# Retention and a SwiGLU feed-forward on one core: where the block sums of the gate and value weights are made, where their rounding keeps its scratch, and which engine writes two diagonals

## The chip, the cores and the metric
The kernel runs on one core of a Trainium2 chip. A core has five engines with a queue of their own each: TensorE (PE, with the load of its weights shown apart as PEld), VectorE (DVE), ScalarE (ACT), GpSimd (POOL) and SyncE (SP), which here does nothing but issue transfers. Every engine works off its instructions in the order in which the program lists them, and waits for others by semaphores. The metric is the device time of one execution in microseconds; less is better.

## The reference
Eight batches of eight heads: a retention block (attention without softmax, with a decay for each head), whose result goes as 4608 rows of 512 into a feed-forward block.

```python
scores = scale * np.matmul(q, k.transpose(0, 1, 3, 2))          # q, k, v: (8, 8, 576, 64)
ret = scores * Dmat[None, :, :, :]                              # decay gamma**(i - j) below the diagonal
x = np.matmul(ret, v).astype(np.float32)                        # then (B*S, H*D) = (4608, 512)
rms = np.sqrt(np.mean(x * x, axis=-1, keepdims=True) + 1e-06)
xn = x / rms * rms_g
g = xn @ w_gate                                                 # (512, 1536)
val = xn @ w_val
return (g * (1.0 / (1.0 + np.exp(-g))) * val @ w_out).astype(np.float32)
```
Of the inputs, the three weight matrices arrive as 64-bit floating point numbers, that is, as two 32-bit words each.

## The kernel before
**Units.** The 4608 rows are nine units of 512. For each, attention makes x (four head pairs, one "job" each: `turn` or `prepare`, `scores`, `states`, `weigh`, `sums`, then `values` and `carried`), a norm follows, then the products with gate and value weights ("up") and those with the output weights (`across`). From the third unit on (`up`, L609), an up product of 2 x 2 blocks takes seven block products in place of eight, which needs four sums of the weight's blocks: S1 to S4, beside A11, A12, A22. Units 0 and 1 (`up_plain`, L668) use the four plain blocks A11, A12, A21, A22 and no sums; they run while the weights are still being prepared.

**Rounding.** [...] They come in 36 halves (L853): 24 of the gate and value weights (six sets of four blocks) and 12 of the output weights (three slices of four). `load_half` brings one half of 512 KB raw into one of `N_RAW` places (three in the ring, two in other buffers). Then, on DVE: `exponent` (L896, one operation), two ScalarE operations (L889), `mantissa` (L911, L915, L919) and `join` (L936), which writes the rounded block. `exponent` of the next half stands ahead of `mantissa` of this one. `weights(n)` lists the next n of these steps; three make a half. In the first seven steps the scratch lies in SBUF; then `in_psum` is set (L1098), and the exponent and the masked high word each take one of the eight PSUM banks. The banks go round in the order of their allocation: who takes one waits for the last user of that bank, eight allocations back. `up_plain` takes one bank for each of its steps (eight matmul instructions), and the evictions by DVE (L685) or ScalarE (L687) free it.

**Sums and stores.** When a set's fourth half is joined, `finish_set` (L949) has POOL make the four sums (`combine_blocks`, L947) in a place behind the sets, and lists the stores of seven blocks to `w_up_d` in DRAM, to be issued by SP a few halves later. `finish_slice` does two levels of the like for the output weights (eight POOL operations).

**The ring.** One buffer of 17408 words for each partition. In `start` it holds the second unit's hidden values, three sets, the sums and three raw places; later the weights of `across` and `up`, streamed from DRAM as "pieces". `refill` (L574) issues a piece on SP as soon as the pieces that it overlaps have been listed as used; the transfer itself waits until they have been read. SP also issues the q, k, v loads of the jobs (`fetch`) and the stores of the output (`store`), all in program order.

**The norm of units 0 and 1.** `norm_1` (L467): four small matmuls and POOL's power give 1/rms for each row; `diagonals` (L480) writes it onto four diagonals by DVE; `scale_x` (L537) spreads them by one matmul into a bank (`rb`) and scales x by four DVE operations. `scale_first` (L265) has POOL scale q and v of the first eight jobs.

The order around this in `start`: four slots of jobs 0 to 3 with a few rounding steps between, the norm of unit 0, the slot of job 4, then 48 steps of `up_plain` in the hand-written order of L1100, with jobs 5 to 7, the norm of unit 1 and three rounding steps at each step (`now` counts them), and `across(0)`, `across(1)`. Then the loop over units 2 to 8 (L1185).

Of the kernel before, what the change touches and what calls it, by code (L numbers as in the profile page):

```python
# [14 lines left out]
P = 128  # L15
# [30 lines left out]
def kernel(  # L46
# [87 lines left out]
    h_1 = ring[:, : NF * U].rearrange("p (f t) -> p f t", t=U)  # L134
    BLOCK = 2 * 2 * P
    AT_SETS, N_SETS = NF * U, 3
    AT_SUMS = AT_SETS + N_SETS * 4 * BLOCK
    AT_RAW = AT_SUMS + 4 * BLOCK
    WORDS = 2 * 4 * P
    assert AT_RAW + 3 * WORDS <= RING  # L140
# [12 lines left out]

# [326 lines left out]
    def diagonals(u):  # L480

        r = t_of[u]
        t_of[u] = row(f"diag_{u}")
        for s in range(NS):
            nc.vector.tensor_scalar(
                out=t_of[u][:, s * P : s * P + P], in0=ident, scalar1=r[:, s : s + 1],
                scalar2=None, op0=ALU.mult,
            )

    def root_1(u):  # L490
# [64 lines left out]


    UP, OUT = 7 * 2 * 2 * P, 7 * NK * P
    w_up_d = dram.tile([2 * NG, P, UP], F32, name="w_up_blocks")
    w_out_d = dram.tile([7, NK, P, 7 * P], F32, name="w_out_blocks")
    ORDER = (A11, S1, S3, S2, A12, S4, A22)  # L560
    pieces = [("out", u, n) for u in range(2) for n in range(7)]
    for u in range(2, NU):
        pieces += [("up", u, n) for n in range(2 * NG)] + [("out", u, n) for n in range(7)]
    places = []
    at = AT_SUMS
    for kind, u, n in pieces:
        size = UP if kind == "up" else OUT
        if at + size > RING:
            at = AT_SETS if kind == "out" and u < 2 else 0
        places.append((at, at + size))  # L570
        at += size
    n_sent = n_used = 0

    def refill(most=len(pieces)):  # L574

        nonlocal n_sent
        while n_sent < min(most, len(pieces)):
            a, z = places[n_sent]
# [9 lines left out]
            nc.sync.dma_start(out=o, in_=src)  # L588
            n_sent += 1

    def piece(kind, u, n):
        assert pieces[n_used] == (kind, u, n) and n_used < n_sent
        a, z = places[n_used]
        if kind == "up":
            return ring[:, a:z].rearrange("p (b c f) -> p b c f", b=7, c=2)
        return ring[:, a:z].rearrange("p (c n d) -> p n c d", n=7, c=NK)

    def used():
        nonlocal n_used
# [68 lines left out]
    def up_plain(u, k):  # L668


        m, f = k % 2, k // 2 * 2
        hh = h_1 if u else h
        w = set_of(k)
        for half in range(2):
            for i in range(2):
                ps = bank(f"up_{u}_{k}_{half}_{i}")
                for c in range(NHP):
                    blk = (A21, A22)[c // 2] if half else (A11, A12)[c // 2]
                    nc.tensor.matmul(  # L679
                        ps, lhsT=w[:, PLACE[blk], c % 2, i * P : i * P + P],  # L680
                        rhs=x_of[u][:, c], start=(c == 0), stop=(c == NHP - 1),
                    )
# [208 lines left out]

    def exponent(i):

        exps[i] = bank(f"exp_{i}") if in_psum else flat_t[i % 2][:, WORDS:]
        w, e = words_of(i), exp_of(i).bitcast(U32)
        nc.vector.tensor_scalar(  # L896
            out=e, in0=w[:, 1::2], scalar1=20, scalar2=0x7FF,
            op0=ALU.logical_shift_right, op1=ALU.bitwise_and,
        )
        f = exp_of(i)  # L900
        acts.extend((i, x) for x in (
            dict(out=f, in_=e, bias=most, scale=-1.0),
            dict(out=e, in_=f, bias=top, scale=-(2.0**23)),
        ))

    def mantissa(i):
# [8 lines left out]
        nc.vector.tensor_scalar(  # L915
            out=m, in0=hi, scalar1=0xFFFFF, scalar2=0x100000,
            op0=ALU.bitwise_and, op1=ALU.bitwise_or,
        )
        nc.vector.scalar_tensor_tensor(  # L919
            out=lo.bitcast(F32), in0=lo, scalar=2.0**-32, in1=m, op0=ALU.mult, op1=ALU.add  # L920
        )

    def join(i):
# [2 lines left out]
        x, e = words_of(i)[:, 0::2].bitcast(F32), exp_of(i)  # L926
        if kind == "up":
            blk = ((A11, A12), (A21, A22))[a][c]
            cuts = [(set_of(k)[:, PLACE[blk]].rearrange("p c f -> p (c f)"), x, e)]
# [18 lines left out]

    def finish_set(k):  # L949
        w = set_of(k)  # L950
        s = ring[:, AT_SUMS : AT_SUMS + 4 * BLOCK].rearrange("p (b c f) -> p b c f", b=4, c=2)
        combine_blocks(
            {i: (w[:, n] if i in (A11, A12, A22, A21) else s[:, n - 3]) for i, n in PLACE.items()},
            A21,
        )
        stores.append((n_joined + 3, [
            (o, t.rearrange("p b c f -> p (b c f)"))
            for o, t in ((w_up_d[k][:, : 3 * BLOCK], w[:, :3]), (w_up_d[k][:, 3 * BLOCK :], s))
        ]))

    def finish_slice(k):
# [10 lines left out]
                nc.sync.dma_start(out=o, in_=t)  # L972

    stores = []
    in_psum = False
    n_joined = 0
    due = False
    sets_used = [0] * 2 * NG
# [44 lines left out]


    def start():

        nonlocal in_psum
# [13 lines left out]
        for j in range(FIRST):  # L1041
# [22 lines left out]
        for j in range(NHP):  # L1064
# [105 lines left out]
        for i, _ in enumerate(across(1)):  # L1170
# [70 lines left out]
```

## Time and profile before
| | |
|---|---|
| runs (4) | median 1157.88 us, 1154.86 to 1160.65 |
| the profiled execution | 1157.71 us, of which the span is 1155.7 us |
| mean granted TensorE clock | 0.982 |
| PE busy | 1105.4 us, 96% |
| PEld busy | 917.8 us, 79% |
| DVE busy | 819.9 us, 71% |
| POOL busy | 426.2 us, 37% |
| ACT busy | 242.6 us, 21% |
| DMA | 249.23 MB, mean 216 GB/s |

The span runs from the first instruction to the last. Its stages: to 53.5 us the first loads, jobs 0 to 4 and the norm of unit 0; to 268 us the plain products of units 0 and 1 with the rounding (done on DVE at 214.5 us); to 344 us `across(0)` and `across(1)`; to about 427 us the up products of the third unit; then the remaining units, each alike. A page row of waits names the engine and line that waited, who released it, the total time, how often, and the longest. Durations of a group are minimum, median and maximum in nanoseconds. The chain that ended last holds only the end of the last unit's combining on DVE (1145 to 1153 us).

### The profile page before, as it was taken

Reading aid. Unit: us, or ns where it says so; the run is one execution under the profiler, and the core shown is the slowest. Engines: PE = TensorE matmul, PEld = TensorE weight load, DVE = VectorE, ACT = ScalarE, POOL = GpSimd, SP = SyncE. Lnnn points to the kernel's source line nnn. Section 1 sums busy time; section 2 is a strip of 40 time slices with the busy share of each in tenths; the row PEclk is TensorE's granted clock in tenths of the full one; section 3 lists DMA queues with packets and bytes.
Section 4 is the critical chain, followed back from the end, with each engine's and each line's share of the span. In section 5 each row is a group of like instructions: output and inputs, shape, how many; then the busy total and the mean of one; then the engine's idle time right before and its main releaser. Section 6 shows DMA issues by size and latency. Waiting matters only on the chain. (4 is left out here: it accounts for less than half of the span.)

```text
span 1155.7 us, 24188 instructions
## 1 busy us (share of the span) xinstructions
PE 1105.4 (96%) x10086; PEld 917.8 (79%) x10086; DVE 819.9 (71%) x1402; ACT 242.6 (21%) x497; POOL 426.2 (37%) x356
## 2 busy tenths in 40 slices
PE   7697999898999999999999999999999999999997
PEld 6453443457998889888988899889988998898897
DVE  3877999466796779577947795779576944593465
ACT  3252453111012130123012301221212111201110
POOL 4522654405652018301740164006500660174035
PEclk9799999898999999999999999999999999999999
DMA  8726889459897887587767974788576566475461
GB/s 194 193 55 179 297 306 285 123 161 297 282 345 239 237 236 259 161 212 209 265 214 212 240 269 183 184 221 303 203 179 223 192 223 216 145 276 174 160 237 39
DMA packets 255612, 249.23 MB, mean 216 GB/s; under 512 B 193296, under 2 KB 214032, under 8 KB 249360
## 3 DMA queue, kind: packets, MB, share of 16 engines
q1 hardware_dynamic: 253776, 247.11, 68.4%
q8 instruction: 79, 1.29, 0.5%
q10 hardware_dynamic: 1728, 0.58, 0.2%
q14 instruction: 29, 0.24, 0.1%
HBM read 217.58 MB, written 30.08 MB: 214 GB/s over the span
## 5 line engine op out<-in xcount | busy, mean ns | idle before, releaser
L730 POOL TENSOR_TENSOR vi<-h 128x384 f32<-128x384 f32 x64 | 79.5, 1259 | 515.1 <-DVE h L637 454.0
L679 PE MATMUL up<-x,ring 128*128 128x512 f32 x384 | 173.5, 608 | 10.4 <-DVE ring L936 9.0
L618 PE MATMUL x<-x,ring 128*128 128x256 f32 x672 | 161.5, 383 | 0.0
L618 PE MATMUL w<-sums,ring 128*128 128x256 f32 x672 | 159.3, 380 | 0.0
L618 PE MATMUL z<-x,ring 128*128 128x256 f32 x672 | 158.7, 379 | 0.0
L679 PEld LDWEIGHTS up<-x,ring 128*128 128x128 f32 x384 | 72.7, 193 | 103.6 <-issue 85.5
L618 PEld LDWEIGHTS z<-x,ring 128*128 128x128 f32 x672 | 127.7, 190 | 19.9 <-issue 2.9
L618 PEld LDWEIGHTS w<-sums,ring 128*128 128x128 f32 x672 | 127.3, 190 | 17.4
L618 PEld LDWEIGHTS x<-x,ring 128*128 128x128 f32 x672 | 125.1, 190 | 17.5
L618 PE MATMUL y<-sums,ring 128*128 128x256 f32 x336 | 79.4, 379 | 0.0
L625 DVE TENSOR_TENSOR h<-u,w 128x512 f32<-128x512 f32 x42 | 28.9, 687 | 66.0 <-PE w L618 62.9
L831 POOL TENSOR_TENSOR vi<-vi 128x512 f32<-128x512 f32 (+1 forms) x56 | 67.2, 1213 | 22.2 <-DVE vi L777 19.7
L618 PEld LDWEIGHTS y<-sums,ring 128*128 128x128 f32 x336 | 63.8, 190 | 8.7
L625 DVE TENSOR_TENSOR u<-m,y 128x512 f32<-128x512 f32 x42 | 28.8, 685 | 49.8 <-PE y L618 49.8
L644 ACT COPY m<-x 128x512 f32<-128x512 f32 x42 | 24.6, 586 | 182.0 <-PE x L618 182.0
L350 DVE SCALAR_TENSOR_TENSOR sum<-sum,gc,s 128x64 f32<-128x64 f32 x192 | 53.9, 281 | 6.8
L639 ACT ACTIVATE h<-h 128x512 f32<-128x512 f32 x63 | 39.5, 629 | 85.0 <-DVE h L625 85.0
L773 ACT COPY vi<-xo 128x512 f32<-128x512 f32 x18 | 10.6, 587 | 211.3 <-PE xo L759 176.9
L947 POOL TENSOR_TENSOR ring<-ring 128x512 f32<-128x512 f32 x24 | 30.5, 1274 | 60.0 <-DVE tick L378 16.3
L947 POOL TENSOR_TENSOR vi<-vi 128x512 f32<-128x512 f32 (+1 forms) x24 | 40.4, 1683 | 30.9 <-issue 14.9
L625 DVE TENSOR_TENSOR u<-u,z 128x512 f32<-128x512 f32 x42 | 28.9, 687 | 26.3 <-PE z L618 25.2
L730 POOL TENSOR_TENSOR vi<-h,vi 128x384 f32<-128x384 f32 x32 | 45.0, 1406 | 2.5
(250 smaller groups left out, 2017.2 us busy)
## 6 DMA issues: line engine op xcount, KB each, us to landing
ring<-w_out_blocks SPq DMA_DIRECT2D x63, 1344.0 KB, 6.6
ring<-w_up_blocks SPq DMA_DIRECT2D x42, 1792.0 KB, 7.8
w_out_blocks<-vi SPq DMA_DIRECT2D x21, 448.0 KB, 4.4
out_dram<-vi SPq DMA_DIRECT2D x64, 128.0 KB, 3.1
qraw<-in_q_dram SPq DMA_DIRECT2D x96, 72.0 KB, 5.4
kraw<-in_k_dram SPq DMA_DIRECT2D x96, 72.0 KB, 3.1
w_up_blocks<-ring SPq DMA_DIRECT2D x6, 1024.0 KB, 9.0
k<-in_k_dram SPq DMA_DIRECT2D x48, 128.0 KB, 2.9
```

Of the source, the lines that this page charges most:

```text
L350: nc.vector.scalar_tensor_tensor(out=t[:, c], in0=t[:, c - 1], scalar=gc[:, hp : hp + 1], in1=part, op0=ALU.mult, op1=ALU.add,)
L618: nc.tensor.matmul(ps[:, i * HU : i * HU + HU], lhsT=w[:, PLACE[blk], c, i * P : i * P + P], rhs=t_of[u][blk][:, c], start=(start and i == ...
L625: nc.vector.tensor_tensor(out=o, in0=a, in1=pairs_of(ps), op=ALU.add)
L639: nc.scalar.activation(out=o, in_=c, func=AF.Silu)
L644: nc.scalar.copy(out=s1, in_=pairs_of(x_))
L679: nc.tensor.matmul(ps, lhsT=w[:, PLACE[blk], c % 2, i * P : i * P + P], rhs=x_of[u][:, c], start=(c == 0), stop=(c == NHP - 1),)
L730: eng.tensor_tensor(out=o, in0=a, in1=b, op=op)
L773: nc.scalar.copy(out=o, in_=ps)
L831: eng.tensor_tensor(out=t[:, :, o], in0=t[:, :, x], in1=t[:, :, y], op=ALU.add)
L947: nc.gpsimd.tensor_tensor(out=t[o], in0=t[x], in1=t[y], op=op)
```

## The change
The four sums of each gate and value set are no longer made in `start`. The stored set has eight places instead of seven (A21 is kept, as the eighth), the four plain blocks alone are stored after rounding, and the third unit (u = 2) loads only these four into a ring place of eight blocks, by two transfers a piece. `new_blocks(n)` has POOL make the sums there: pieces 0 and 1 during `across(1)` (after its fifth and sixth products), and piece n + 1 during the up product n, for n from 1 to 4. `store_new_blocks(n)` then has SP store the four sums, and units 3 to 8 load seven blocks as before. The place of the sums in the ring becomes two more raw places, so seven halves can be under way. The rounding's scratch stays in SBUF throughout. The diagonals are written by ScalarE copies with a scale for each partition. In `start` some rounding steps are listed at other points.

```diff
-    AT_SUMS = AT_SETS + N_SETS * 4 * BLOCK
-    AT_RAW = AT_SUMS + 4 * BLOCK
+    AT_RAW = AT_SETS + N_SETS * 4 * BLOCK
...
-    spare = [ring[:, AT_RAW + i * WORDS : AT_RAW + i * WORDS + WORDS] for i in range(3)]
+    spare = [ring[:, AT_RAW + i * WORDS : AT_RAW + i * WORDS + WORDS] for i in range(5)]
     spare += [t[:, :WORDS] for t in flat_t]
...
-    PLACE = {A11: 0, A12: 1, A22: 2, S1: 3, S2: 4, S3: 5, S4: 6, A21: 3}
+    PLACE = {A11: 0, A12: 1, A22: 2, S1: 3, S2: 4, S3: 5, S4: 6, A21: 7}
+    IN_SET = {A11: 0, A12: 1, A22: 2, A21: 3}
...
     def diagonals(u):
-            nc.vector.tensor_scalar(
-                out=t_of[u][:, s * P : s * P + P], in0=ident, scalar1=r[:, s : s + 1],
-                scalar2=None, op0=ALU.mult,
+            nc.scalar.activation(
+                out=t_of[u][:, s * P : s * P + P], in_=ident, func=AF.Copy, scale=r[:, s : s + 1]
             )
...
-    w_up_d = dram.tile([2 * NG, P, UP], F32, name="w_up_blocks")
+    w_up_d = dram.tile([2 * NG, P, 8 * BLOCK], F32, name="w_up_blocks")
...
-    at = AT_SUMS
+    at = AT_RAW
-        size = UP if kind == "up" else OUT
+        size = OUT if kind == "out" else 8 * BLOCK if u == 2 else UP
...
     def refill(most=len(pieces)):
             if kind == "up":
-                src = w_up_d[n]
+                src = w_up_d[n][:, : z - a]
+                if u == 2:
+                    for cut in (slice(0, 3 * BLOCK), slice(7 * BLOCK, 8 * BLOCK)):
+                        nc.sync.dma_start(out=o[:, cut], in_=src[:, cut])
+                    n_sent += 1
+                    continue
...
+    def new_blocks(n):
+        i = pieces.index(("up", 2, n))
+        assert n_used <= i < n_sent
+        w = blocks_at(*places[i])
+        combine_blocks([w[:, PLACE[b]] for b in range(8)], A21)
+
+    def store_new_blocks(n):
+        a, _ = places[pieces.index(("up", 2, n))]
+        cut = slice(3 * BLOCK, 7 * BLOCK)
+        nc.sync.dma_start(out=w_up_d[n][:, cut], in_=ring[:, a + cut.start : a + cut.stop])
...
     def exponent(i):
-        exps[i] = bank(f"exp_{i}") if in_psum else flat_t[i % 2][:, WORDS:]
+        exps[i] = flat_t[i % 2][:, WORDS:]
...
     def mantissa(i):
-        m = bank(f"man_{i}").bitcast(U32) if in_psum else hi
         nc.vector.tensor_scalar(
-            out=m, in0=hi, scalar1=0xFFFFF, scalar2=0x100000,
+            out=hi, in0=hi, scalar1=0xFFFFF, scalar2=0x100000,
...
     def finish_set(k):
-        combine_blocks(
-            {i: (w[:, n] if i in (A11, A12, A22, A21) else s[:, n - 3]) for i, n in PLACE.items()},
-            A21,
-        )
-        stores.append((n_joined + 3, [
-            (o, t.rearrange("p b c f -> p (b c f)"))
-            for o, t in ((w_up_d[k][:, : 3 * BLOCK], w[:, :3]), (w_up_d[k][:, 3 * BLOCK :], s))
+        stores.append((n_joined + 2, [
+            (w_up_d[k][:, b * BLOCK : (b + n) * BLOCK], w[:, i : i + n].rearrange("p b c f -> p (b c f)"))
+            for b, i, n in ((0, 0, 3), (7, 3, 1))
         ]))
...
     def start():
             elif j == 7:
-                load_half(4, nc.sync)
+                for i in range(4, N_RAW):
+                    load_half(i, nc.sync)
...
             if j == 2:
                 weights(1)
                 act(2)
-            elif j == 3:
-                weights(1)
         close(NHP - 1)
         gather(*squares.pop())
         squared(0, NHP - 1)
-        act(2)
-        weights(2)
+        weights(3)
         gather(*squares.pop(), nc.vector)
         turn(NHP)
         norm_1(0)
+        diagonals(0)
         weights(2)
-        diagonals(0)
-        weights(1)
         scores(NHP)
         states(NHP)
         weigh(NHP)
         norm_2(0)
+        weights(1)
         sums(NHP)
         scale_first(NHP + 1)
         turn(NHP + 1)
         scale_first(NHP + 2)
-        in_psum = True
...
         for i, _ in enumerate(across(1)):
             elif i == 8:
                 norm_2(2)
                 sums_of_x(2)
+            elif i == 10:
+                new_blocks(0)
+            elif i == 12:
+                new_blocks(1)
...
                 for i, _ in enumerate(up(u, n)):
+                    if u == 2 and i == 1 and 0 < n < 2 * NG - 1:
+                        new_blocks(n + 1)
+                    if u == 2 and i == 5:
+                        store_new_blocks(n)
```

More of the change, by code (lines that the diff above doesn't have):

```diff
@@ L136 @@
     AT_SETS, N_SETS = NF * U, 3
-    AT_SUMS = AT_SETS + N_SETS * 4 * BLOCK
-    AT_RAW = AT_SUMS + 4 * BLOCK
+    AT_RAW = AT_SETS + N_SETS * 4 * BLOCK
     WORDS = 2 * 4 * P
-    assert AT_RAW + 3 * WORDS <= RING
+    assert AT_RAW + 5 * WORDS <= RING
     flat_t = [t1.rearrange("p f t -> p (f t)"), sums_x.rearrange("p i c t -> p (i c t)")]
-    spare = [ring[:, AT_RAW + i * WORDS : AT_RAW + i * WORDS + WORDS] for i in range(3)]
+    spare = [ring[:, AT_RAW + i * WORDS : AT_RAW + i * WORDS + WORDS] for i in range(5)]
     spare += [t[:, :WORDS] for t in flat_t]
@@ L594, in piece, with blocks_at @@
         if kind == "up":
-            return ring[:, a:z].rearrange("p (b c f) -> p b c f", b=7, c=2)
+            return blocks_at(a, z)
         return ring[:, a:z].rearrange("p (c n d) -> p n c d", n=7, c=NK)
+    def blocks_at(a, z):
+        return ring[:, a:z].rearrange("p (b c f) -> p b c f", b=(z - a) // BLOCK, c=2)
+    def new_blocks(n):
[7 more added lines that the diff above has]
+        nc.sync.dma_start(out=w_up_d[n][:, cut], in_=ring[:, a + cut.start : a + cut.stop])
     def used():
@@ L679, in up_plain @@
                     nc.tensor.matmul(
-                        ps, lhsT=w[:, PLACE[blk], c % 2, i * P : i * P + P],
+                        ps, lhsT=w[:, IN_SET[blk], c % 2, i * P : i * P + P],
                         rhs=x_of[u][:, c], start=(c == 0), stop=(c == NHP - 1),
@@ L919, in mantissa @@
         nc.vector.scalar_tensor_tensor(
-            out=lo.bitcast(F32), in0=lo, scalar=2.0**-32, in1=m, op0=ALU.mult, op1=ALU.add
+            out=lo.bitcast(F32), in0=lo, scalar=2.0**-32, in1=hi, op0=ALU.mult, op1=ALU.add
         )
@@ L928, in join @@
             blk = ((A11, A12), (A21, A22))[a][c]
-            cuts = [(set_of(k)[:, PLACE[blk]].rearrange("p c f -> p (c f)"), x, e)]
+            cuts = [(set_of(k)[:, IN_SET[blk]].rearrange("p c f -> p (c f)"), x, e)]
         else:
@@ L950, in finish_set @@
         w = set_of(k)
-        s = ring[:, AT_SUMS : AT_SUMS + 4 * BLOCK].rearrange("p (b c f) -> p b c f", b=4, c=2)
-        combine_blocks(
-            {i: (w[:, n] if i in (A11, A12, A22, A21) else s[:, n - 3]) for i, n in PLACE.items()},
-            A21,
-        )
-        stores.append((n_joined + 3, [
-            (o, t.rearrange("p b c f -> p (b c f)"))
-            for o, t in ((w_up_d[k][:, : 3 * BLOCK], w[:, :3]), (w_up_d[k][:, 3 * BLOCK :], s))
+        stores.append((n_joined + 2, [
+            (w_up_d[k][:, b * BLOCK : (b + n) * BLOCK], w[:, i : i + n].rearrange("p b c f -> p (b c f)"))
+            for b, i, n in ((0, 0, 3), (7, 3, 1))
         ]))
@@ L974 @@
     stores = []
-    in_psum = False
     n_joined = 0
@@ L1025, in start @@
     def start():
-        nonlocal in_psum
         tables = list(zip((causal, gv, gc, gq, gx, gf), (_causal_table(), *_decay_tables(H, D))))
```

## The prediction
> **What bounds the kernel now.** The profiled execution took 1157.71 us, its span 1155.7, so 2.0 us lie around the span; the median of the runs is 1157.88. The page's busy times give PE 96% of the span: no edit can win more than PE's idle 50 us, and part of that is the first loads. So I read who made PE wait, then in which stretch.
>
> ```profile
> PE up L679 <- DVE ring L936: 9.0, 6, 4.4
> PE rb L537 <- DVE diag L485: 6.9, 1, 6.9
> PE wo L759 <- DMA ring<-w_out_blocks: 4.0, 1, 4.0
> PE s L321 <- DVE sums L919: 3.8, 1, 3.8
> ...
> 103.16 79.22 PE L679 MATMUL up<-x,ring 128*128 128x512 f32 x180 [4.42 <-DVE ring L936]
> ...
> 110.00:200.00 90.00, 87.76 (x203) 37.76 (x202) 86.53 (x146) 39.57 (x64) 45.85 (x31) 1.00 0.88 294
> 200.00:220.00 20.00, 16.19 (x102) 7.74 (x101) 12.02 (x27) 6.03 (x12) 7.75 (x7) 0.83 0.51 151
> ```
> The first four lines are PE's waits (total us, times, longest). Three of them end on the rounding or on the diagonals. The last two are stretches (busy us of PE, PEld, DVE, ACT, POOL, then clock, DMA share, GB/s): from 110 to 200 us DVE is 96% busy, beside PE. Behind 290 us PE hardly waits, so the change is worth what it does before, less its cost at the third unit (344 to 427 us).
>
> Next, what one DVE operation of the rounding costs with its scratch in PSUM and in SBUF (durations min/median/max in ns):
> ```profile
> L896 DVE TENSOR_SCALAR exp<-ring x19: 666/687/695, 80.0 to 208.4; 128x512 uint32<-128x512 uint32 x19
> L896 DVE TENSOR_SCALAR t<-ring x2: 417/422/426, 26.5 to 39.9; 128x512 uint32<-128x512 uint32 x2
> L915 DVE TENSOR_SCALAR ring<-ring x2: 428/1080/1732, 33.6 to 41.0; 128x512 uint32<-128x512 uint32 x2
> L919 DVE SCALAR_TENSOR_TENSOR ring<-ring,man x20: 687/689/706, 65.3 to 213.0; 128x512 f32<-128x512 uint32 x20
> L919 DVE SCALAR_TENSOR_TENSOR ring<-ring x2: 1414/1532/1650, 35.3 to 41.5; 128x512 f32<-128x512 uint32 x2
> L936 DVE SCALAR_TENSOR_TENSOR ring<-ring,t x2: 691/692/693, 37.0 to 66.0; 128x512 f32<-128x512 f32 x2
> ...
> 121.13 12.69 POOL L947 TENSOR_TENSOR vi<-vi 128x512 f32<-128x512 f32 x7 [5.39 <-DVE vi L936]
> ```
> Wholly in SBUF the two one-input operations are quicker (0.42 for 0.69), and the two-input ones cost the same 0.69 while POOL rests, but 1.4 to 1.65 while POOL runs. With PSUM scratch none is disturbed. So the sign hangs on how often POOL runs beside the rounding. The last line is its longest stretch.
>
> **The change, part by part.**
>
> Start, 35 to 53.5 us. The four diagonals took 5.93 us on DVE, since POOL's scalings ran beside them (one took 3.17, against 0.28 at best), and PE waited 6.9. On ScalarE four copies cost 4 x 0.34 = 1.4 (by L282, 0.335 for 64x64 and 0.50 for 128x256). POOL's power ends at 41.5, or 0.4 later because one exponent now stands before the square's sum; the diagonals are done at 43.4 and PE has its product at 45.5 instead of 50.9. That is 5.4 us, but a new wait takes most of it. The ScalarE work of half 1 now stands behind the diagonals: 43.4 + 0.75 + 0.72 = 44.9, where it was done at 37.7. DVE's three mantissa operations wait for it and run beside POOL until 50: 3.7 (1.3 + 1.0 + 1.4) to 5.7 (with one stalled like the 3.17 row), to 48.6 or 50.6; then the weighing 0.85, x's scaling 2.7, the join 0.7. Half 1 is ready at 52.9 to 54.9, and the first up product, which needs it after its first two passes (1.7 us), ends at 54.6 to 56.6 where it ended at 57.15. Gain 0.5 to 2.5; I take 1.5, and -0.5 as the bad end, should DVE stall twice.
>
> 53 to 103 us. A half's rounding starts its operations 0.60, 0.60, 0.72, 0.72 and 0.60 us apart (121 to 124 us); two become 0.34 and 0.46, so it takes 2.72 for 3.24. POOL's sums of sets 0 and 1 (8 x 1.27 us) are gone, so little stands beside it. At 72 us PE's 1.48 shrinks by some 0.9. At 91 us the diagonals leave DVE (0.8), half 6 gains 0.5 and half 7 gains 0.5, and x's scaling starts earlier: DVE reaches the join that PE awaits at 103.16 some 2.6 us sooner. Gain 3.5, between 1.5 and 5.
>
> 103 to 235 us. PE's step here is 3.44 (x24 in 10.57 less x16 in 7.13 us, 8 matmuls a step). From 103.16 to 206.5 it makes 228/8 = 28.5 steps, 98.0 us, so 5.3 are lost in small waits; then 3.8 for L919, and 2.0 in the next six steps (22.87 for 20.9), where the granted clock mean is 0.83 behind that idle. In all 11.1. Why does PE wait at all, when rounding is emitted five or more halves ahead of its use? Because the scratch takes two of the eight PSUM banks in rotation for each half: the lines of who waits on bank writers name L919 and the exponents, and the 3.8 is PE asking for the bank of a mantissa, which DVE had not begun because its raw half landed 5.1 us late. Both causes go: no scratch in PSUM, and with seven places all raw loads are queued ahead of the attention loads that held SP up at 187.7 us. What remains is DVE's total: 28 halves x 2.75 = 77, 14 products x 0.6 = 8.4, two transposes 1.4, in all 87 against PE's 96. To this comes POOL: two slices of weights are still combined beside it (1.28 + 12.69 us each). With one DVE operation to each POOL operation at 1.5 us, 14 us pass 9.3 of them, 1.9 halves where 5.1 would pass: 8.8 us lost, twice, 17.6. If the one-input operations stall for 3.17 it is 10.5, twice. Then DVE ends 8 to 12 us behind PE. Five steps (17 us) cover that; if the cover is gone, PE pays what exceeds it, and then the products at L685 hold banks again. With DVE as the bound the stage would last 104.6 to 108, against 103.4 + 3.8 = 107.2 now. Gain between -0.8 and 11.1; I take 9, near the upper row, since the lag stays under the cover.
>
> The Trainium skill (SBUF — State Buffer, "Who interferes with whom") speaks against this part: a VectorE instruction with two SBUF inputs, or a one-input one in a two-port mode, shares a lock with GpSimd, and the later one waits out the other's whole instruction. The rows of 1.41 to 1.65 and 3.17 agree. By the rule every rounding operation beside POOL would wait for one POOL instruction; as an estimate from that page the loss per slice lies near the larger one above, and the forecast stands.
>
> SP and POOL while rounding: 24 POOL sums (30.5 us) leave; the stores shrink from seven blocks a set to four. Hidden, worth nothing by itself.
>
> Third unit. The sums return to POOL: six times four, 4 x 1.27 = 5.1 us each. POOL is free from 337.3, the first piece (1 MB now, for 1.75) lands near 340 (some 5.5 us behind its issue at 334.3; 7.8 is the median for 1.75 MB), so the first sums run 340 to 345.1 beside DVE's four differences of x (0.69 each alone, 1.24 to 1.27 beside POOL in other units): 2.3 us longer. PE wants the third of both at 345.6; they come at 343.8 and 344.9. Cost 0 to 3; I take 0.5. POOL then does the second piece's sums to 350.3, and the output's combining ends at 359 instead of 354.7; its store was issued at 371. The later sums lie in POOL's idle time of 41 us (345 to 396 but for the combining). SP gets six stores of 1 MB (9.0 us to landing when DMA was full) and the refills over the same places must wait for them: behind these stand the q, k and v loads of the next head pair. By my reckoning the fetch of 379.5 starts near 384.5, but that of before then took 16 us for what costs 6.7 to issue, as 3.1 MB lay ahead of it in the queues; now 1 MB does, and it ends no later.
> ```profile
> 379.45 8.64 SPq L164 DMA_DIRECT2D qraw<-in_q_dram  x4
> ...
> SPq L588 <- PE w L618: 20.5, 2, 12.1
> ```
> So I cost the stores at nothing, with SP's waits on PE (the second line, of 330 to 430 us) as cover. The output weights' 4.0 wait at 282 us rests on the order of loads in SP, which the change leaves; it stays.
>
> Sum: 1.5 + 3.5 + 9 - 0.5 = 13.5 off 1157.7, so 1144.2, I say 1144.
>
> **Rivals.** *DVE stays the bound through POOL.* For it: the 1.5 and 3.2 us rows, and slack that I only reckoned. Against it: POOL is left with 28 us there. Then 103 to 235 gives 107.2 - 104.6 = 2.6: 1157.7 - 1.5 - 3.5 - 2.6 + 0.5 = 1151.
>
> *The stores hold up SP in the third unit*, slower than before. SP waits for each store to land before its refill, the next head pair's loads come late, DVE's transposes wait in order, and PE behind them. For it: six landings of 9.0 us are 54, and SP's waits on PE there are 20.5 + 4.7 + 4.7 + 3.5 = 33. Against it: less is loaded. If nothing else covers them, 21 us are lost: 1144.2 + 21 = 1165. It decides once more than 13.5 us reach PE.
>
> *All waits go*: 5.4 + 5 + 11.1 + 2.5 at 282 us, 1134. For it: the clock recovers with shorter gaps. Against it: half 1's late work.
>
> *It doesn't do what it says*: PE's losses at 103 to 206 are not of the banks, and the start loses what the middle wins, 1157.
>
> **Chances.** Forecast 0.50 (own range 1138 to 1149), DVE bound 0.22 (1150 to 1156), stores 0.16, all waits 0.07, nothing 0.05. Faster by over 0.3% (below 1154.4; 0.3% is about what this kernel's measurement can tell from none): 0.50 + 0.07 + three quarters of 0.22 = 0.73. Within: 0.05 + 0.05 = 0.10. Slower: 0.17, the stores and a trace of the last. The range runs from 1134 to 1160: it leaves out most of the stores' case and a little below.
>
> **What would show it.** No wait of PE on L919; the 79 us row at 3.44 us a step; L915 and L896 near 0.42 but for two clusters beside POOL's L947; the rb product near 44 and a new wait of the first up product on DVE; POOL's sums in the ring from 340 us. Wrong, if PE's waits on L936 grow, or SP's refills wait on the stores and the transposes or v's scaling on loads in the third unit.

## The result, and the profile after

The changed kernel takes 1160.87 us (median of 42 runs, 1155.06 to 1166.71) where the kernel before takes 1158.36 (63 runs): a ratio of 1.0028, 95% interval 1.0017 to 1.0038 (worked out from all the runs, so not the quotient of the two medians). The forecast was 1144, faster; it came out a little slower. The profiled execution has a span of 1159.1 us against 1155.7, at nearly the same mean clock (0.984 and 0.982).

Divided at the same instructions of PE in both traces, the 3.4 us of the spans come about so (us; a gain is positive; the borders are the last `carried` product of job 3, the end of the first up product, the wait at 103 us, the last product of `start`, and the first products of the third unit's first and second set):

| stretch | before | after | predicted gain | gain |
|---|---|---|---|---|
| to job 3 | 32.97 | 35.35 | none | -2.4 |
| to the end of the first up product | 24.24 | 23.41 | 1.5 | 0.8 |
| to 103 us | 45.95 | 44.41 | 3.5 | 1.5 |
| to 268 us | 164.55 | 164.42 | 9 | 0.1 |
| `across(0)` and `across(1)` | 76.18 | 74.43 | 0 | 1.8 |
| the third unit's first set | 13.39 | 17.64 | -0.5 | -4.3 |
| the rest | 798.42 | 799.44 | 0 | -1.0 |

The table compares one execution of each kernel, and some rows hold chance. In the other kernels below the last product of job 3 begins anywhere between 32.35 and 35.22 us, and the two passes of `across` last 72.5 to 77.1 us in those with the changed kernel's ring, so the -2.4 and the 1.8 are no effects to build on. Two rows hold the result: nothing of the 9 us arrived, and the third unit cost 4.3 instead of 0.5.

The waits of PE up to 360 us in the changed kernel (us in all, times, longest), to be laid beside those of before:

```profile
PE up L699 <- DVE x L538: 6.2, 1, 6.2
PE up L699 <- DVE ring L955: 5.8, 2, 4.0
...
PE up L699 <- DVE ring L705: 3.1, 1, 3.1
...
PE y L638 <- DVE sums L550: 2.3, 1, 2.3
...
PE rb L536 <- ACT diag L485: 1.6, 1, 1.6
```

Most lines of the code stand 19 or 20 lower than before (L679 is L699, L936 is L955, L685 is L705). The wait on L919 is gone and that on the diagonals is down from 6.9 to 1.6, both as meant. In their place stand the scaling of x (6.2) and, new, the products of the up pass, L705.

The stretches of before again, in the changed kernel (us, then busy us of PE, PEld, DVE, ACT, POOL with their instruction counts, then clock, DMA share, GB/s):

```profile
110.00:200.00 90.00, 90.00 (x211) 39.87 (x210) 87.29 (x122) 37.65 (x58) 30.45 (x16) 1.00 0.65 224
200.00:220.00 20.00, 12.12 (x90) 5.65 (x89) 19.25 (x36) 10.54 (x18) 1.45 (x1) 0.74 0.73 213
```

PE is busy without a gap to 200 us, as forecast: its slot of job 8 begins at 201.22, where before it began at 206.45. Then it stands still for 8 of 20 us, and its clock falls to 0.74. DVE, 97% busy from 110 to 200 us (96% in the kernel before), is the reason. This is the slot, on PE, and then the products of DVE that hold up its banks (start, us, engine, line, what, idle time before it and its releaser):

```profile
195.55 5.74 PE L699 MATMUL up<-x,ring 128*128 128x512 f32 x13
201.22 0.81 PE L301 MATMUL s<-qT,kT 64*64 64x64 f32 x40
204.19 0.77 PE L321 MATMUL s<-v,k 64*64 64x64 f32 x28 [2.15 <-issue]
207.59 0.48 PE L321 MATMUL last<-v,k 64*64 64x64 f32 x4 [2.64 <-DVE ring L705]
211.17 11.01 PE L699 MATMUL up<-x,ring 128*128 128x512 f32 x18 [3.09 <-DVE ring L705]
...
203.40 0.68 DVE L705 TENSOR_TENSOR ring<-ring,up 128x512 f32<-128x512 f32 x1
206.86 0.68 DVE L705 TENSOR_TENSOR ring<-ring,up 128x512 f32<-128x512 f32 x1
210.43 0.68 DVE L705 TENSOR_TENSOR ring<-ring,up 128x512 f32<-128x512 f32 x1
```

Each wait of PE ends as one of these three products ends (204.08, 207.54, 211.11); for the first the view names no releaser, only "issue". The banks go round in eight, so the slot's third score bank, its `last` bank and the next up step's bank are those of steps 29, 30 and 31 of the 48. Counted back from the end of step 34 (201.3) at 3.43 us a step, PE had filled them by 184.1, 187.6 and 191.0. DVE empties them 20 us later.

### The profile page after: what moved, and what is told of

It is laid out like the page before. It is cut to its first block, busy times and chain, and to the rows that moved or that the text cites. A ratio compares the mean times of both kernels' runs of the same rounds, so it can differ in the third digit from the quotient of the medians.

```text
span 1159.1 us, 24240 instructions
## 1 busy us (share of the span) xinstructions
PE 1105.2 (95%) x10086; PEld 918.6 (79%) x10086; DVE 834.1 (72%) x1394; ACT 248.6 (21%) x505; POOL 433.2 (37%) x356
## 5 line engine op out<-in xcount | busy, mean ns | idle before, releaser
L699 PE MATMUL up<-x,ring 128*128 128x512 f32 x384 | 173.0, 609 | 15.1 <-DVE x L538 6.2
L699 PEld LDWEIGHTS up<-x,ring 128*128 128x128 f32 x384 | 73.6, 195 | 106.9 <-issue 91.3
L638 PEld LDWEIGHTS x<-x,ring 128*128 128x128 f32 x672 | 125.2, 190 | 18.5 <-issue 1.1
L966 POOL TENSOR_TENSOR vi<-vi 128x512 f32<-128x512 f32 (+1 forms) x24 | 44.0, 1835 | 94.8 <-DVE vi L955 82.4
L851 POOL TENSOR_TENSOR vi<-vi 128x512 f32<-128x512 f32 (+1 forms) x56 | 67.2, 1213 | 13.8 <-DVE vi L797 11.3
L334 DVE SCALAR_TENSOR_TENSOR ret<-s,causal 128x320 f32<-128x320 f32 x64 | 28.4, 484 | 23.8 <-PE s L301 23.3
```

The source lines that it names most:

```text
L334: nc.vector.scalar_tensor_tensor(out=ret[:, e], in0=s[e][:, : n * L].rearrange("p (c k) -> p c k", k=L), scalar=float(_gamma(H)[2 * hp + e ...
L638: nc.tensor.matmul(ps[:, i * HU : i * HU + HU], lhsT=w[:, PLACE[blk], c, i * P : i * P + P], rhs=t_of[u][blk][:, c], start=(start and i == ...
L699: nc.tensor.matmul(ps, lhsT=w[:, IN_SET[blk], c % 2, i * P : i * P + P], rhs=x_of[u][:, c], start=(c == 0), stop=(c == NHP - 1),)
L851: eng.tensor_tensor(out=t[:, :, o], in0=t[:, :, x], in1=t[:, :, y], op=ALU.add)
L966: nc.gpsimd.tensor_tensor(out=t[o], in0=t[x], in1=t[y], op=op)
```

## The experiments

All times are medians; ratios are to the kernel before on the same chip, from all the runs, with 95% intervals. The traces are of one execution each. "The changed kernel" stands at 1.0028.

**Without the slices' sums.** POOL's sums of slices 0 and 1 are left out; so that their places are written, ScalarE fills them once with ones.

```diff
     def finish_slice(k):
-        combine_blocks([slices[:, i, :4] for i in range(7)], S1)
-        combine_blocks([slices[:, :, i] for i in range(7)], S1)
+        if k == 2:
+            combine_blocks([slices[:, i, :4] for i in range(7)], S1)
+            combine_blocks([slices[:, :, i] for i in range(7)], S1)
...
                     diagonals(1)
+                    for o in range(7):
+                        to = slices[:, o, 4 if o < 4 else 0 :]
+                        nc.scalar.activation(
+                            out=to, in_=ones.unsqueeze(1).to_broadcast([P, to.shape[1], P]), func=AF.Copy
+                        )
```

> The changed kernel (1160.9) with POOL's sums of the first two output-weight slices left out (their places are filled once by ScalarE instead), so that POOL hardly runs beside the rounding. Theory A, the lag: each of these two stretches of POOL holds DVE up by 11 us, and PE pays at the slot of job 8, where it waits 7.9 us for banks that DVE's products hold. Then the waits at 201 to 211 us go, and the stage from PE's 103 us to its 235 us shrinks from 131.8 to about 123: 1152 in all (1150 to 1154). Rival B, the banks: DVE's own work or the order in which banks are taken holds PE there whatever POOL does: 1159 to 1161, with the waits of some 8 us still at job 8.

Measured: 1150.73, ratio 0.994 (0.9919 to 0.9961). The waits at job 8 are gone. POOL's sums beside the rounding (31.4 us in the changed kernel) are what PE paid for.

**Scratch back in PSUM from half 3.**

```diff
     def exponent(i):
-        exps[i] = flat_t[i % 2][:, WORDS:]
+        exps[i] = bank(f"exp_{i}") if i > 2 else flat_t[i % 2][:, WORDS:]
...
     def mantissa(i):
...
+        m = bank(f"man_{i}").bitcast(U32) if i > 2 else hi
...
-            out=hi, in0=hi, scalar1=0xFFFFF, scalar2=0x100000,
+            out=m, in0=hi, scalar1=0xFFFFF, scalar2=0x100000,
...
-            out=lo.bitcast(F32), in0=lo, scalar=2.0**-32, in1=hi, op0=ALU.mult, op1=ALU.add
+            out=lo.bitcast(F32), in0=lo, scalar=2.0**-32, in1=m, op0=ALU.mult, op1=ALU.add
```

> The changed kernel with the rounding's scratch back in PSUM from half 3 on; sums in the third unit, seven raw places and ScalarE diagonals stay. Theory A: no DVE operation is held up by POOL; a half costs 3.25 us again and PE is tied to DVE by the banks (some 5 us lost in small waits), but the raw halves no longer come late, so the 3.8 us wait and the clock behind it go: 126 us for the stage, 1155 in all (1153 to 1157). Rival C, SBUF scratch is the gain and POOL's stalls are hidden: as slow as the changed kernel or slower, 1160 to 1165.

Measured: 1150.51, ratio 0.9937 (0.9913 to 0.9961). Of the rivals the one that held the scratch in SBUF to be the gain falls: taking it back is worth 0.9%. It takes two banks a half again, and yet PE waits on no product of L705 and loses only 0.9 us from 103 to 200 us; the loss of some 5 us that was expected there did not come, and the time lies below the 1153 to 1157 expected.

**PSUM only beside the slices' sums** (halves 12 to 16 and 24 to 28).

```diff
-        exps[i] = bank(f"exp_{i}") if i > 2 else flat_t[i % 2][:, WORDS:]
+        exps[i] = bank(f"exp_{i}") if i in (12, 13, 14, 15, 16, 24, 25, 26, 27, 28) else flat_t[i % 2][:, WORDS:]
...
-        m = bank(f"man_{i}").bitcast(U32) if i > 2 else hi
+        m = bank(f"man_{i}").bitcast(U32) if i in (12, 13, 14, 15, 16, 24, 25, 26, 27, 28) else hi
```

The diff is against the experiment before.

> The changed kernel with the scratch in PSUM for ten halves alone (12 to 16 and 24 to 28), those that are rounded while POOL sums a slice. Theory A: the 2.2 us operations beside POOL become 0.69, DVE's lag of some 20 us shrinks to under 5, the waits at job 8 go: 1152 (1150 to 1155). Rival B: 1159 to 1161, waits at job 8 as before. If the banks taken in these halves tie PE to DVE, a loss of some 2 us inside the two stretches shows in PE's pace (3.44 us a step without).

Measured: 1151.61, ratio 0.9935 (0.991 to 0.996). The same stretches of DVE show the mechanism by itself. First the changed kernel beside POOL's sums, with the scratch in SBUF:

```profile
119.88 1.76 DVE L931 SCALAR_TENSOR_TENSOR t<-t 128x512 uint32<-128x512 uint32 x1
121.68 1.38 DVE L934 TENSOR_SCALAR t<-t 128x512 uint32<-128x512 uint32 x1
...
124.77 2.45 DVE L955 SCALAR_TENSOR_TENSOR ring<-t 128x512 f32<-128x512 f32 x1
127.25 2.19 DVE L916 TENSOR_SCALAR t<-ring 128x512 uint32<-128x512 uint32 x1
129.36 2.57 DVE L931 SCALAR_TENSOR_TENSOR sums<-sums 128x512 uint32<-128x512 uint32 x1
...
119.65 14.21 POOL L966 TENSOR_TENSOR vi<-vi 128x512 f32<-128x512 f32 x7 [5.74 <-DVE vi L955]
```

Then this experiment, with scratch in PSUM, beside the same sums, and its two stretches from 110 to 220 us:

```profile
116.35 0.68 DVE L931 SCALAR_TENSOR_TENSOR exp<-t,exp 128x512 uint32<-128x512 uint32 x1
116.95 0.68 DVE L935 TENSOR_SCALAR man<-t 128x512 uint32<-128x512 uint32 x1
...
115.98 12.69 POOL L967 TENSOR_TENSOR vi<-vi 128x512 f32<-128x512 f32 x7 [5.86 <-DVE vi L956]
...
110.00:200.00 90.00, 90.00 (x280) 40.27 (x279) 86.94 (x152) 43.05 (x67) 27.46 (x17) 1.00 0.76 252
200.00:220.00 20.00, 20.00 (x77) 8.84 (x78) 7.23 (x17) 2.24 (x6) 12.12 (x7) 1.00 0.31 58
```

In SBUF seven operations of DVE fill the 14.2 us in which POOL makes seven of its own, and POOL itself takes 14.21 for 12.69. In PSUM every one takes 0.68 or 0.69, and from 200 to 220 us PE is busy throughout, at the full clock. (The profiled execution was the fastest of eight, 1144.46.) The busy shares hide the difference, since an operation that is held counts as busy: from 110 to 200 us DVE is busy for 87.29 us with 122 operations in the one kernel and for 86.94 with 152 in the other.

**ScalarE's work of half 1 ahead of the diagonals**, in the changed kernel.

```diff
         weights(3)
+        act(2)
         gather(*squares.pop(), nc.vector)
```

> The changed kernel with the two ScalarE operations of half 1 listed ahead of the diagonals instead of behind them. Theory D: DVE's first mantissa operation of half 1, held up 3.6 us by ScalarE and then 4.3 us long beside POOL, runs near 42 us in 0.7 to 1.5; the first up product ends near 55 instead of 58.7, and all behind it moves by 3: 1158 (1156 to 1159). Rival E: the two-input operations just meet POOL's scalings elsewhere, or x's scaling is the later one anyway: within 1 us of 1160.9, the first up product still ending at 58 or later.

Measured: 1157.17, ratio 0.9993 (0.9972 to 1.0013), 3.7 us below the changed kernel's median. The changed kernel first, ScalarE and DVE:

```profile
42.81 1.28 ACT L485 ACTIVATE diag<-ident,r 128x128 f32<-128x128 f32 x4 [1.87 <-POOL r L477]
...
45.49 4.29 DVE L931 SCALAR_TENSOR_TENSOR sums<-ring,sums 128x512 uint32<-128x512 uint32 x1 [3.60 <-ACT sums L909]
```

And with the one line moved:

```profile
40.56 0.68 DVE L931 SCALAR_TENSOR_TENSOR sums<-ring,sums 128x512 uint32<-128x512 uint32 x1
```

The mantissa's first operation now runs before POOL's scalings begin, 0.68 us in place of a wait of 3.60 and a run of 4.29 beside them. The first up product ends at 51.8 instead of 58.8, but 3.0 us of this is an earlier job 3 (32.35 for 35.35), and the changed kernel's trace is a late case: in the four other kernels that keep its order up to there the product ends at 52.6 to 57.0, in those with the line moved at 51.3 to 54.5. The 3.7 us of the medians are the better measure. The waits at job 8 stay (2.1, 2.6 and 3.1): a stage that starts earlier with the same lag ends earlier by as much.

**The third unit's x scaled two passes earlier.**

```diff
-            elif i == 8:
+            elif i == 6:
                 norm_2(2)
+            elif i == 8:
                 sums_of_x(2)
```

> The changed kernel with one edit: the third unit's x is scaled by VectorE two passes earlier (ahead of the last four inner sums), so that its four operations no longer stand beside the first eight sums of GpSimd. Theory U (the third unit lost 4.2 us because these eight sums run beside VectorE's scaling and differences of x, 4.76 and 6.5 us where they took 2.73 and 2.9): the wait of the product y on the differences (2.3) goes or falls under 0.5, the first seven products take 13.4 to 14 us instead of 17.6, and the time is 1157 (1155.5 to 1158). Rival V (the lateness is of the weights' landing or of the piece's larger size, 2.0 us of GpSimd's wait on the transfer): the stretch stays near 17 and the time near 1160.9.

Measured: 1159.14, ratio 1.0018 (0.9999 to 1.0037). The time expected, 1155.5 to 1158, was missed. The mechanism is seen, in the changed kernel:

```profile
337.40 12.84 POOL L966 TENSOR_TENSOR ring<-ring 128x512 f32<-128x512 f32 x8 [2.02 <-DMA ring<-w_up_blocks]
...
336.31 4.76 DVE L538 SCALAR_TENSOR_TENSOR x<-x,rms_k,sq 128x512 f32<-128x512 f32 x4
341.11 1.64 DVE L550 TENSOR_TENSOR sums<-x 128x512 f32<-128x512 f32 x1
...
346.23 3.04 PE L638 MATMUL y<-sums,ring 128*128 128x256 f32 x8 [2.32 <-DVE sums L550]
```

and in this one:

```profile
329.37 2.74 DVE L538 SCALAR_TENSOR_TENSOR x<-x,rms_k,sq 128x512 f32<-128x512 f32 x4
338.08 0.69 DVE L550 TENSOR_TENSOR sums<-x 128x512 f32<-128x512 f32 x1
...
345.76 1.89 PE L638 MATMUL y<-sums,ring 128*128 128x256 f32 x8
```

The wait of y is gone and the set takes 13.40 us (344.03 to 357.43), as before the change. But the set begins 2.0 us later than in the changed kernel. On the way the trace shows 1.2 us of waiting on an output piece at 314 us and 0.6 on inner sums near 336 that the changed kernel does not have, and lacks a wait of 1.5 on GpSimd's inner sum that it has; so this accounts for a part of the 2.0 only. Theory U holds for the wait and its 4.2 us; what the edit wins in the time, some 1 to 2 us, can't be told from nothing, as the intervals overlap.

**Three edits together**: PSUM beside the slices' sums, ScalarE's work first, x scaled early.

> The changed kernel with three edits: scratch of the rounding in PSUM for the halves beside the slices' sums only, the ScalarE work of half 1 ahead of the diagonals, and the third unit's x scaled earlier. If the three losses (slice sums beside rounding, the order at the start, the third unit) are separate, their gains add up: 1160.9 - 9.3 - 3.7 - 3.9 = 1144, which is the prediction's 1144.0. If they overlap (an earlier start only makes VectorE's lag behind PE larger, so the gain is waited away at about 200 us), it is 1148 to 1152.

Measured: 1147.45, ratio 0.9908 (0.9889 to 0.9927). This lies between the two times expected (1144, and 1148 to 1152). Against the changed kernel the three ratios alone add up to 0.0093 + 0.0035 + 0.0010 = 0.0138; together they are worth 0.0120. So the losses are nearly separate, as far as the intervals tell, and most of the forecast's gain was there to be had. From the wait at 98.71 to the last product of `start` at 253.97 PE takes 155.3 us where it took 164.55 before: 9.3 us, the 9 of the forecast.

**The kernel before, with its rounding in SBUF throughout.**

```diff
-        in_psum = True
```

> The kernel before with the scratch of its rounding in SBUF throughout, nothing else. Theory A (VectorE's two-input operations in SBUF are what GpSimd delays): here GpSimd also makes 24 sums of gate and value blocks beside the rounding, 6 sets of some 5 us, so VectorE loses two slices' 10 us each and some 3 us a set; the lag appears at PE by 100 us and the time is 1170 to 1185. Theory C (SBUF scratch is the gain, the slices alone are the harm): near the changed kernel, 1158 to 1164.

Measured: 1173.5, ratio 1.0122 (1.0101 to 1.0143). Two of PE's waits behind 90 us:

```profile
PE s L301 <- DVE kT L261: 7.4, 1, 7.4
PE up L679 <- DVE ring L685: 5.8, 1, 5.8
```

This part of the change, made on its own, costs 1.2%; here it also meets POOL's 24 sums of gate and value blocks, which the changed kernel has moved away. Where the text expected the lag at PE by 100 us it was wrong: the wait that ends at 103.55 is 4.10, against 4.42 before, and DVE's lag reaches PE only at 195 us and then at job 8's slot (214 us). There it is so long that even the transposes of k are late.

**The kernel before, with the diagonals by ScalarE alone.**

```diff
     def diagonals(u):
-            nc.vector.tensor_scalar(
-                out=t_of[u][:, s * P : s * P + P], in0=ident, scalar1=r[:, s : s + 1],
-                scalar2=None, op0=ALU.mult,
+            nc.scalar.activation(
+                out=t_of[u][:, s * P : s * P + P], in_=ident, func=AF.Copy, scale=r[:, s : s + 1]
             )
```

> The kernel before with the diagonals made by ScalarE, nothing else; its ScalarE work for half 1 stands ahead of the diagonals already. Theory D (the diagonals are worth what the first up product gains, if the exponent's ScalarE work does not stand behind them): PE's wait of 6.9 us on the diagonals falls to 1 to 2, the first up product ends 2 to 4 us earlier, and the time is 1154.5 to 1157. Rival: VectorE's later waits at 72, 91 and 103 us take it back, 1158.

Measured: 1151.08, ratio 0.9936 (0.9918 to 0.9954), better than expected. Two of its waits of PE:

```profile
PE s L321 <- DVE sums L918: 4.2, 1, 4.2
...
PE rb L536 <- ACT diag L485: 1.4, 1, 1.4
```

The first up product ends at 52.1 instead of 57.2, the last product of `start` begins at 262.66 instead of 267.71. The five microseconds are carried through every later wait, that on the mantissa's bank (4.2) among them, and to the end.

**As the three edits, but with PSUM scratch from half 3 on.**

> As the run with the three losses mended, but with the rounding's scratch in PSUM from half 3 on, as the kernel before has it, and not only beside the slices' sums. If scratch in SBUF is worth something where GpSimd rests (halves 3 to 11 and 17 to 23), this is slower than 1147.5 by the 0.5 us a half that the prediction reckoned, 3 to 6 us where PE waits on them, 1150 to 1154. If it is worth nothing (PE's waits at 70, 97 and 103 us are of something else, and VectorE has slack behind 103), it is 1146 to 1149, and the change's gain beside the diagonals is the sums' move alone.

Measured: 1146.35, ratio 0.9893 (0.9876 to 0.991), not to be told from the 0.9908 of PSUM beside the sums only. Scratch in SBUF wins nothing where POOL rests, although its two one-input operations are 0.26 us shorter each: DVE has time there (it waits 13.1 us for PE's products between 100 and 230 us). This has the lowest median of the study, ahead of both kernels.

**The same, with the third unit's stores issued four passes earlier.**

```diff
-                    if u == 2 and i == 5:
+                    if u == 2 and i == (1 if n else 5):
                         store_new_blocks(n)
```

> The kernel with PSUM scratch throughout, the ScalarE work first and x scaled early, and one edit more: SyncE issues the third unit's stores of the new blocks four passes earlier, so that they have landed when their places are refilled. The changed kernel's SyncE waited 33 us in all on these landings. Rival stores (they also cost PE the 1.3 to 2.4 us that the fourth unit loses near 523 us against the kernel before): SyncE's waits on the landings fall below 15 us, the loss goes, 1 to 2 us faster than the run beside it. Otherwise (the loss is of the ring's new order, in which an output piece is loaded ahead of the head pair's q and k): the waits fall and the time stays.

Measured: 1150.31, ratio 0.9924 (0.9905 to 0.9943), slower than the run beside it by 4.0 us (the intervals just touch). SP's longest row of waits on the stores, first in the changed kernel, then here:

```profile
SPq L592 <- DMA w_up_blocks<-ring: 21.0, 4, 8.1
```

```profile
SPq L592 <- DMA w_up_blocks<-ring: 7.0, 1, 7.0
```

The changed kernel's SP waits 25 us in all on these landings (21.0 and 4.0 at another line; the 33 of the expectation counts 8.1 of them twice), here 8.1. The waits fell by two thirds and nothing was won. What the fourth unit's fourth set loses against the kernel before (1.1 us in the changed kernel, 1.4 to 2.4 in the others before this one that have its ring) is not SP's waiting on stores. Here the third unit's third set and the fourth unit's fourth set, from the second product of one to that of the next, together last 36.3 us, against 33.1 in the run beside it and 30.8 before. Whether that is the transfers' company or the order of the ring's pieces stays open.

**The same as two before, with five raw places in place of seven.**

```diff
-    spare = [ring[:, AT_RAW + i * WORDS : AT_RAW + i * WORDS + WORDS] for i in range(5)]
+    spare = [ring[:, AT_RAW + i * WORDS : AT_RAW + i * WORDS + WORDS] for i in range(3)]
```

> The kernel with PSUM scratch throughout, the ScalarE work first and x scaled early (1146.4), with five places for raw halves, as the kernel before has, in place of seven. The prediction put PE's 3.8 us at the slot of job 8 (near 206 us) down to a raw half that landed late because its load stood behind the attention's loads in SyncE's queue. If that holds, the wait on a mantissa's bank comes back at job 8, 3 to 4.2 us, VectorE waits some 5 us for a raw half near 195 us, and the time is 1149.5 to 1151. Rival: with GpSimd's sums of gate and value blocks gone from the rounding the loads are early enough with five places too; no wait, and 1145 to 1148.

Measured: 1150.65, ratio 0.9957 (0.9938 to 0.9976), outside the interval with seven places (0.9876 to 0.991). Two of PE's waits behind 104 us that come with it:

```profile
PE up L699 <- DVE ring L956: 1.5, 1, 1.5
PE s L321 <- DVE sums L939: 0.8, 1, 0.8
```

DVE's longest wait for a raw half is 2.1 us (5.1 in the kernel before; with seven places it has none). The direction is the forecast's, the size of the wait is not: it is less than the 3 to 4.2 that were expected. The stretch from the wait near 97 us to the last product of `start` is 160.6 us, against 156.7 with seven places. Seven places are worth 4 us by the medians, 7 by the ratios; in this ring it is the move of the sums that makes room for them.

## Why the prediction was wrong, step by step

**The step that failed is the cover in 103 to 235 us.** The prediction had DVE ending "8 to 12 us behind PE. Five steps (17 us) cover that; if the cover is gone, PE pays what exceeds it, and then the products at L685 hold banks again". The mechanism, and the place where PE would pay, were named; both sizes were wrong. The first three experiments show that POOL's sums, through the lag of DVE, made PE stand still at job 8.

- *The lag.* The loss for each slice was put at 8.8 to 10.5 us. Seven operations that take 4.2 us without POOL (from 149.81 to 153.98 in the same trace) took 14.3, so 10.1, and the lone sum ahead of them cost 1.1 more: 11.2 in all, above the upper end, since POOL's 128x896 sums cost DVE 2.2 to 2.6 each where 1.5 was taken. The slack set against it was too large as well. A half alone takes 2.98 us with its scratch in SBUF (149.47 to 152.45) where 2.72 was reckoned, and the whole slack of the stage (96 less 87 us) was set against both losses. It can't be spent so: ahead of the first sums DVE can't run ahead of PE (at 105.19 it waits 2.08 us for PE's product), and in passes with a product at each step DVE needs 3.45 us a step (its products of steps 24 to 27 begin at 184.81, 188.27, 191.72 and 195.17), as much as PE. So little of the first slice's lag is made good: DVE empties a bank some 10 us after PE has filled it behind the first slice, 18.5 behind the second, and 20 at job 8, not 8 to 12.
- *The cover.* Five steps is right for the first of the banks on which PE waits, and only for that one. The slot of job 8 takes four banks at one point of PE's order, so the next two banks asked for were filled four and three steps earlier, 10 us at the least. PE then waits as each of three products comes, 2.2 + 2.6 + 3.1 = 7.9 us, and its clock falls behind them (0.74 from 200 to 220 us, 0.83 before). This takes back what the 98.1 us from 103 to job 8, forecast as 98.0, had won.

**What was right in that stage.** PE's small losses to 206 us did go (28.6 steps at 3.43), L919 and the raw load's 5.1 did go, and the cause that the prediction gave for the raw load holds in part: five places bring back some of it. But the banks were not the brake that they were taken for: with PSUM scratch from half 3 on the stage to 268 us takes 156.7 us, with PSUM beside the slices' sums alone 155.3, so the banks cost some 1.4. With the scratch where POOL can't delay it the stage gives 9.3, the predicted 9 by another way than the one predicted: the 9 itself was chosen near the upper end of a range of 11.9, not summed. Of the 7.9 us won with PSUM scratch throughout, five raw places give 3.9 back; where the other 4.0 come from, no run tells.

**The weighing of the rule.** The Trainium skill (SBUF — State Buffer, "Who interferes with whom") says that a VectorE instruction with two SBUF inputs, or a one-input one in a two-port mode, waits out the whole of a GpSimd instruction that reads SBUF and came first. The prediction let this stand beside its own bound. The rows agree with it (1.38 to 2.57 us a piece beside POOL, 0.68 to 0.69 with an operand in PSUM), but two go beyond it: the 4.29 us at 45.49, through six of GpSimd's instructions, and the 3.17 us that the prediction counted as agreeing, though no scaling beside it took more than 1.04. The larger error was not in the rule but in the slack set against it.

**Start.** The diagonals were done at 44.1 us and PE's product at 45.3, near the 43.4 and 45.5 reckoned, and the new wait on ScalarE's work came too (3.60). The gain of 0.8 lies within the range given; in the four other kernels with this order the same stretch takes 19.7 to 23.3 us for 23.4, so one trace can't test a forecast of 1.5. But the prediction took the order as it found it and so missed that the part alone is worth 6.5 us: undone by one line, the order gives back 3.7 in the changed kernel.

**53 to 103 us.** 1.5 for 3.5, the low end of its range. The wait of 1.2 us at 97 went. The one near 75 us grew to 1.8 (1.5 before, near 73), where 0.9 was to go, and at 103 PE still waits 4.0 us for 4.4 (4.0 to 4.3 in the kernels of the study). There the working took DVE for the bound, but the scaling of x, which stands ahead of the join that PE awaits, now waits for PE's own `rb` product: it begins 1.1 us behind that product's start, 2.6 before. So what DVE saves ahead of it does not all pass on.

**Third unit.** 4.3 for 0.5. The working had DVE's differences slowed by 2.3 us from POOL's sums, but not the scaling of x: the first piece had landed by 337.4 us where 340 was reckoned, and the sums lay beside the scaling too (4.76 for 2.73). And it put each difference at 1.24 to 1.27, means that include the undisturbed 0.69, where 1.64 was measured. So y waited 2.3 us, and the next two products took 3.04 and 2.55 us for 1.89.

**The rivals.** "DVE stays the bound through POOL" (1151) was the case, and too mild: it had the same slack in it. The stores' rival had the sign of the result and is not its cause: SP waited 25 us in all on their landings, and the fetch reckoned for 384.5 began at 384.86; but behind the third unit's first set PE lost 1.0 us net, and earlier stores did not win it back.

**The parts, alone.** Diagonals by ScalarE -0.64%; rounding in SBUF +1.22% in the kernel before; the sums' move with five places, PSUM scratch, the diagonals and the mended start and third unit -0.43%, which is no better than the diagonals alone, so the move by itself wins nothing that shows; the two more places that it makes room for, some -0.6%. Between the changed kernel and the fastest the ratios differ by 0.0135; the scratch beside POOL's sums is 0.0093 of it, the order at the start 0.0035.

## What to carry to other kernels

A lag is covered by the buffers that stand free at the point where the consumer asks, not by the steps of the whole stage: look for the place where several buffers are taken at once. Slack of a stage can pay for a stall only behind it, and only where the program lists work ahead; sum it from the stall on. Before VectorE work is moved from PSUM to SBUF, list what GpSimd does beside it (here the one-input operations were held too, 2.18 and 2.19 us for 0.43), and when a helper's work changes engines, look at what stands ahead of it in that engine's order.

## What the runs showed of the hardware

- Beside GpSimd, one operation of DVE can be held for longer than one of GpSimd's: 4.29 us at 45.49, while GpSimd ran six scalings of 0.39 to 1.04 us one after another. The same operation in the same order took 1.56, 1.56, 1.57 and 3.28 us in four other kernels, and 0.68 or 0.69 where it ran ahead of the scalings, so the price of one such meeting varies by several microseconds.
- GpSimd pays too: its seven sums took 14.21 us against 12.69 beside an undisturbed DVE.
- After the 8 us of waits on PE near 205 us the next 48 matmuls took 23.9 us, where 20.87 is their time in the runs without those waits. The granted clock was 0.50 from 207.6 to 215.0 us and 1.00 again from 220; over 200 to 220 us it was 0.74, for 1.00 without the waits. So these waits cost 3 us more than their length.
